# Reordering the loads and turns of the first two batches in an attention-and-MLP kernel

## The chip, the cores and the metric

The kernel runs on one core of a Trainium2 chip. The metric is device time in microseconds (us), the median of several executions. The profile's span, from the first to the last instruction, is about 1.7 us shorter than the time of its execution (303.1 and 301.4 for the kernel before).

Engines: PE is TensorE, DVE VectorE, ACT ScalarE, POOL GpSimd, SP SyncE, which here only issues transfers. PEld is PE's loading of weights. In a line of a profile, `L216` is a line of the kernel, `SPq` or `ACTq` an issue of a transfer by that engine, and the bracket says how long the engine was idle before and what ended that.

## The reference

```python
k_p = k.reshape(B, H, Sp, 8, D).mean(axis=3)      # keys pooled by 8; B=8, H=8, S=576, D=64
v_p = v.reshape(B, H, Sp, 8, D).mean(axis=3)
attn = softmax(q @ k_p.T / sqrt(D))               # 576 queries x 72 pooled keys a head
x = (attn @ v_p) reshaped to (4608, 512)
h = x @ w_in                                      # 512 x 2048
out = (h - tanh(h)) @ w_out                       # 2048 x 512
```

## The kernel before

The kernel works through eight batches. Attention of batch b+1 is slipped between the MLP matmuls of token group b. Only the start differs: batch 0's attention (the preamble) has no MLP to hide behind, and batch 1's attention, hidden behind the output matmuls of group 0, needs its data while all the weights are still loading.

k and v of a batch are 144 rows by 4 head pairs. 128 rows are loaded in one piece, and the 16 rows per pair left over (the "leftovers") separately. q is loaded as 4 x 128 rows, and its last 64 rows (the "small pieces", 512 runs of 256 B) separately. "Turning" is a transpose on PE by a matmul with the identity. `warm_pe` issues matmuls of zeros that only keep PE busy. The MLP's weights w_in and w_out (w1 and w2 in the code) are loaded in four pieces each. `KB` holds the turned keys, `VB` the pooled and masked values. AV is the product of the exponentials E with VB.

The preamble and the issue order of loads (cut):

```python
    load_main(k_pairs, k_raw[0], 0, 2, 4)      # SP queue
    load_q0(4, 8)                              # ACT queue
    load_dense(k_pairs, k_raw[0], 0)           # SP queue: leftovers
    load_dense(v_pairs, v_raw[1], 0)
    # ...
    for c in range(4):
        load_w1(c)                             # POOL queue, cast to bf16
    load_w2(0)
    nc.gpsimd.tensor_copy(out=v_bf[:, NM, :], in_=v_raw[1][:, NM, :])
    for c in range(1, 4):
        load_w2(c)
    # ...
    after(load_k(1), w1_dmas[1])               # k of batch 1 waits for the second w1 load
    load_q(1)                                  # main part and small pieces, SP queue
    load_main(v_pairs, v_raw[1], 1, 0, NM)
    # ...
    q_turn(nc.scalar.copy, 4, 6); q_turn(nc.scalar.copy, 6, 8)
    pool_k(0, nc.vector, 2, 4); pool_k(0, nc.vector, NM, NT)
    warm_pe(6)
    q_pe_transpose(0, (2, 3), "act")
    warm_pe(4)
    k_turn(2, 4)
    warm_pe(3)
    k_turn_left()
    v_left(...); vs = v_pe_pool(0, NM, ident); v_main(...)
    scores_wide(0, (NM, 2, 3))
```

Batch 1 behind the output matmuls of group 0 (cut):

```python
    pool_k(1, nc.gpsimd)
    q_cast(1)                                  # POOL
    after(load_k(2), w2_dmas[2])
    for u in range(16):
        qd, tb = u // 4, u % 4
        mlp_o(0, tb, qd * 4, qd * 4 + 4, gts, o_pools[tb])      # output block u
        if u == 0: k_transpose(1, ps_any)
        if u == 3: q_pe_transpose(1, (0, 1))
        # ... q turns at 4, 5; scores at 4 to 8
        if u == 7: pool_v(1, nc.vector)
        # u >= 9: AV of batch 1
```

The softmax here doesn't subtract the row's maximum and nothing guards it: scores larger than these inputs give would overflow.

## Time and profile before

| | |
|---|---|
| time | 303.22 us median (302.86 to 303.46, 4 runs) |
| span | 301.4 us |
| PE busy | 291.6 us, 97% |
| first output block of group 0 | 36.15 us |
| first AV of batch 1 | 49.01 us |
| first hidden block of group 1 | 57.31 us |

These three events cut the kernel into four stretches. The table of busy time has, for each stretch, its length, then busy time and instruction count of PE, PEld, DVE, ACT and POOL, and at the end the granted clock, the DMA share and GB/s. The second and third stretch before:

```profile
36.15:49.01 12.86, 11.75 (x83) 5.80 (x81) 6.88 (x11) 5.59 (x11) 2.49 (x2) 1.00 1.12 314
49.01:57.31 8.30, 8.26 (x74) 5.20 (x75) 6.41 (x23) 3.32 (x6) 7.07 (x4) 1.00 0.87 245
```

### The profile page before, as it was taken

To read this page: it belongs to the slowest core of one execution; us is meant where nothing else is said; L and a number is where in the kernel's file an instruction comes from. 1 tells how busy PE (TensorE), PEld (TensorE's weight loads), DVE (VectorE), ACT (ScalarE), POOL (GpSimd) and SP (SyncE) were. 2 spreads that over 40 slices of the span, in tenths; PEclk is the share of its full clock that TensorE was granted. 3 is DMA by queue.
4 is the path that set the end of the run, shared out by engine and by line. 5 is a ranking of instruction groups with operands and counts; after the bars stand their busy time and mean duration, and the time that the engine had idled before them with its cause. 6 is when DMAs were issued, how large, how long until landed. Compare 5 with 4: busy or idle time off the path is not lost.

```text
span 301.4 us, 4695 instructions
## 1 busy us (share of the span) xinstructions
PE 291.6 (97%) x1672; PEld 142.7 (47%) x1672; DVE 160.1 (53%) x344; ACT 146.4 (49%) x279; POOL 117.9 (39%) x112
## 2 busy tenths in 40 slices
PE   8789998999999999999999999999999999999994
PEld 3354454544554455445544554445444544444443
DVE  5567728685347524862577166807570757107600
ACT  5458642565426642665175506660675156226511
POOL 8701634871297109921991079408930000000000
PEclk9999999999999999999999999999999999999998
DMA  7999999649854896789657975795531430111032
GB/s 260 213 221 276 239 314 324 214 88 327 212 114 88 261 319 130 112 275 251 107 110 206 312 165 114 242 311 128 100 73 35 88 97 0 37 70 35 3 70 70
DMA packets 66183, 49.79 MB, mean 165 GB/s; under 512 B 39920, under 2 KB 52976, under 8 KB 66160
## 3 DMA queue, kind: packets, MB, share of 16 engines
q1 hardware_dynamic: 59520, 43.34, 54.5%
q0 software_dynamic: 4752, 4.72, 9.3%
q10 hardware_dynamic: 1888, 1.44, 1.8%
q8 instruction: 13, 0.21, 0.3%
q14 instruction: 10, 0.08, 0.1%
HBM read 36.70 MB, written 9.44 MB: 153 GB/s over the span
## 4 chain that ended last, share of the span: by engine, by line
PE 81%; DMA 14%; POOL 1%; DVE 1%; issue 0%; ACT 0%; SPq 0%; POOLq 0%
PE o_ps L449 37%; PE hT_ps L421 37%; DMA v_raw<-in_v_dram 6%; PE x_ps L339 4%; DMA w1b<-in_moe_w_in_dram 4%; DMA k_raw<-in_k_dram 3%; PE s_ps L291 3%; DMA out_dram<-o_sb 1%; DVE v_raw L209 0%; PE xT_ps L383 0%; POOL v_raw L569 0%; DVE v_raw L212 0%; DVE VB L223 0%; POOL w1b L496 0%; POOL mask L558 0%
## 5 line engine op out<-in xcount | busy, mean ns | idle before, releaser
L449 PE MATMUL o_ps<-w2b,gT 128*128 128x512 bf16 x560 | 134.4, 380 | 0.0
L434 DVE TENSOR_TENSOR gT<-hT_ps,t_sb 128x512 bf16<-128x512 f32 x144 | 98.9, 691 | 58.9 <-ACT t_sb L432 58.7
L421 PE MATMUL hT_ps<-xT,w1b 128*128 128x512 bf16 x576 | 127.0, 379 | 0.7 <-ACT xT L390 0.7
L432 ACT ACTIVATE t_sb<-hT_ps 128x512 f32<-128x512 f32 x144 | 85.6, 597 | 38.2 <-PE hT_ps L421 37.4
L421 PEld LDWEIGHTS <-w1b 128*128 128x128 bf16 x576 | 55.9, 98 | 66.9 <-issue 1.0
L449 PEld LDWEIGHTS <-gT 128*128 128x128 bf16 x560 | 52.5, 98 | 52.0 <-issue 1.4
L458 ACT COPY o_sb<-o_ps 128x512 f32<-128x512 f32 x33 | 19.3, 585 | 75.2 <-PE o_ps L449 75.2
L352 DVE RECIPROCAL rden<-x_ps 128x4 f32<-128x4 f32 x80 | 14.1, 177 | 50.5 <-PE x_ps L339 50.1
L144 POOL CAST q_bf<-q_raw 128x2048 bf16<-128x2048 f32 x7 | 13.2, 1888 | 62.7 <-DMA out_dram<-o_sb 23.6
L353 DVE TENSOR_TENSOR x_sb<-x_ps,rden 128x256 bf16<-128x256 f32 x80 | 34.0, 424 | 2.8
L193 POOL TENSOR_TENSOR k_raw<-k_raw 128x1280 f32<-128x1280 f32 x7 | 20.2, 2892 | 21.0 <-DMA k_raw<-in_k_dram 21.0
L310 ACT ACTIVATE E<-s_ps 128x288 bf16<-128x288 f32 x60 | 21.4, 410 | 13.2 <-PE s_ps L291 13.0
L339 PE MATMUL x_ps<-VB,E 128*128 128x130 bf16 x240 | 21.0, 221 | 1.1 <-DVE VB L223 1.1
L339 PEld LDWEIGHTS <-E 128*128 128x128 bf16 x240 | 16.9, 98 | 9.6 <-DVE VB L223 1.6
L209 POOL TENSOR_TENSOR v_raw<-v_raw 128x1280 f32<-128x1280 f32 x6 | 17.4, 2902 | 0.0
L291 PE MATMUL s_ps<-qT,KB 128*128 128x288 bf16 (+5 forms) x128 | 16.8, 290 | 0.0
L291 PEld LDWEIGHTS <-KB 128*128 128x128 bf16 (+1 forms) x128 | 7.0, 96 | 10.1 <-issue 3.4
L520 PE MATMUL warm_ps<-xT 128*128 128x512 bf16 x30 | 10.2, 463 | 1.3 <-DVE xT L532 1.3
L199 POOL TENSOR_TENSOR kd<-k_raw 128x640 bf16<-128x640 f32 x7 | 10.8, 1539 | 0.6
L196 POOL TENSOR_TENSOR k_raw<-k_raw 128x640 f32<-128x640 f32 x7 | 10.8, 1537 | 0.5
L390 ACT CAST xT<-xT_ps 128x256 bf16<-128x256 f32 (+1 forms) x14 | 6.0, 434 | 8.4 <-PE xT_ps L383 7.4
L212 POOL TENSOR_TENSOR v_raw<-v_raw 128x640 f32<-128x640 f32 x6 | 9.2, 1540 | 0.5
(73 smaller groups left out, 99.3 us busy)
## 6 DMA issues: line engine op xcount, KB each, us to landing
k_raw<-in_k_dram SPq DMA_DIRECT2D x7, 1024.0 KB, 5.8
q_raw<-in_q_dram SPq DMA_DIRECT2D x7, 1024.0 KB, 10.2
v_raw<-in_v_dram SPq DMA_DIRECT2D x7, 1024.0 KB, 8.9
out_dram<-o_sb SPq DMA_DIRECT2D x38, 128.0 KB, 2.5
out_dram<-o_sb SPq DMA_DIRECT2D x16, 256.0 KB, 2.6
w1b<-in_moe_w_in_dram POOLq DMA_DIRECT2D x4, 512.0 KB, 13.6
w2b<-in_moe_w_out_dram POOLq DMA_DIRECT2D x4, 512.0 KB, 26.8
k_raw<-in_k_dram SPq DMA_DIRECT2D x8, 128.0 KB, 6.0
```

What stands on the lines that cost most here:

```text
L193: first = eng.tensor_tensor(out=r[:, :, 0:4, :], in0=r[:, :, 0:4, :], in1=r[:, :, 4:8, :], op=ALU.add)
L209: eng.tensor_tensor(out=r[:, :, 0:4, :], in0=r[:, :, 0:4, :], in1=r[:, :, 4:8, :], op=ALU.add)
L291: nc.tensor.matmul(dst[p : p + w], lhsT=KB[b % 2][:, o : o + w], rhs=qTs[b][:, m, c0:c1], start=True, stop=True,)
L310: nc.scalar.activation(out=E[:, t, half * hs : (half + 1) * hs], in_=ps[:, :], func=ACT.Exp, scale=SCALE)
L339: nc.tensor.matmul(ps[:, 2 * n : 2 * n + 2, :].rearrange("p h d -> p (h d)") if n < 2 else ps.rearrange("p (a s) d -> p a s d", s=2)[:, :, ...
L352: nc.vector.reciprocal(out=rden[:, :, :], in_=ps[:, :, D:D1])
L353: nc.vector.tensor_tensor(out=x_sb[:, half, :, :], in0=ps[:, :, 0:D], in1=rden[:, :, :].to_broadcast([128, 4, D]), op=ALU.mult,)
L421: nc.tensor.matmul(h_tiles[i][:, :], lhsT=w1b[:, fb, i * 128 : (i + 1) * 128], rhs=xT[:, fb, tok0 : tok0 + TG], start=(fb == 0), stop=(fb ...
L432: nc.scalar.activation(out=t_sb[:, :], in_=h_ps[:, :], func=ACT.Tanh)
L434: nc.vector.tensor_sub(out=gT[:, :], in0=h_ps[:, :], in1=t_sb[:, :])
L449: nc.tensor.matmul(o_ps[:, :], lhsT=gts[i][:, tb * 128 : (tb + 1) * 128], rhs=w2b[:, i, :], start=(i == 0), stop=(i == NHID - 1),)
L458: (nc.vector.tensor_copy if g == 0 and tb % 2 else nc.scalar.copy)(out=o_sb[:, :], in_=o_ps[:, :])
```

## The change

It has two halves. In the preamble, the leftovers of batch 0 are to load behind q, so that q comes sooner, and the second half of k is turned ahead of q. For batch 1, q's small pieces go to the ACT queue, two weight loads are deferred into the pooling of k, q is cast on ScalarE, and the order of the turns follows. Cut to its core:

```diff
-    load_dense(k_pairs, k_raw[0], 0)
-    load_dense(v_pairs, v_raw[1], 0)
+    load_dense(k_pairs, k_raw[0], 0, nc.scalar)
+    load_dense(v_pairs, v_raw[1], 0, nc.scalar)
-    for c in range(1, 4):
-        load_w2(c)
+    load_w2(1)
-    load_q(1)
+    load_q(1, False)                     # without the small pieces
     pool_k(0, nc.vector, 2, 4)
+    warm_pe(6)
+    k_turn(2, 4)
     pool_k(0, nc.vector, NM, NT)
-    warm_pe(6)
+    warm_pe(2)
     q_pe_transpose(0, (2, 3), "act")
-    warm_pe(4)
-    k_turn(2, 4)
-    warm_pe(3)
+    warm_pe(2)
+    scores_wide(0, (2, 3))
     k_turn_left()
     # leftover scores now ahead of v's pooling; two warm_pe(2) more
     load_left(v_pairs, v_raw[1], 1, nc.scalar)
+    load_q_tail(1, q_raws[1], nc.scalar)
+    x_pe_transpose(0, 2, xs[2], (2, 4))
+    x_pe_transpose(0, 3, xs[3], (2, 4))
     mlp_h_mms(0, 3, 0, 2, (ps_o, "o_ps"))
-    x_pe_transpose(0, 2, xs[2], (2, 4))
     mlp_h_mms(0, 4, 0, 2, (ps_o, "o_ps"))
-    x_pe_transpose(0, 3, xs[3], (2, 4))
-    pool_k(1, nc.gpsimd)
-    q_cast(1)
+    pool_k(1, nc.gpsimd, mid=(2, 3))     # w2 loads 2 and 3 issued behind its first add
         if u == 0:
-            k_transpose(1, ps_any)
+            q_cast(1, nc.scalar.copy, 2)
+        if u == 2:
+            k_transpose(1, ps_any, (nc.vector.tensor_copy, nc.vector.tensor_copy))
         # q turns evicted by ACT alone; pool_v(1) at u == 4 instead of 7
```

More of the change, by code (lines that the diff above doesn't have):

```diff
@@ L108, in load_left, with load_dense @@
         ]
-    def load_dense(src, dst, b):
-        return nc.sync.dma_start(
+    def load_dense(src, dst, b, eng=nc.sync):
+        return eng.dma_start(
             out=dst[0 : NM * LO, NM, :], in_=src[b, 128:PR, :, :]
@@ L124, in load_v, with load_q_tail, load_q, q_cast @@
         )
-    def load_q(b, nh=1):
-        t = raw.tile([128, H, R + 1, D], FP32, name="q_raw", tag="q_raw")
-        n = H // nh
-        for i in range(nh):
-            nc.sync.dma_start(
-                out=t[:, i * n : (i + 1) * n, 0:R, :],
-                in_=q[b, i * n : (i + 1) * n, 0:QA, :].rearrange("h (p j) d -> p h j d", j=R),
-            )
-        nc.sync.dma_start(
+    def load_q_tail(b, t, eng):
+        eng.dma_start(
             out=t[:QT, :, R, :], in_=q[b, :, QA:S, :].rearrange("h p d -> p h d")
         )
-        q_raws[b] = t
+    def load_q(b, tail=True):
+        if b not in q_raws:
+            q_raws[b] = raw.tile([128, H, R + 1, D], FP32, name="q_raw", tag="q_raw")
+        t = q_raws[b]
+        nc.sync.dma_start(
+            out=t[:, :, 0:R, :], in_=q[b, :, 0:QA, :].rearrange("h (p j) d -> p h j d", j=R)
+        )
+        if tail:
+            load_q_tail(b, t, nc.sync)
     qTs = {}
     kdups = {}
-    def q_cast(b):
+    def q_cast(b, eng=nc.gpsimd.tensor_copy, parts=1):
         t = q_raws.pop(b)
-        nc.gpsimd.tensor_copy(
-            out=q_bf[:, 0:R, :, :].rearrange("p j h d -> p h j d"), in_=t[:, :, 0:R, :]
-        )
-        nc.gpsimd.tensor_copy(out=q_bf[:QT, R, :, :], in_=t[:QT, :, R, :])
+        n = H // parts
+        for h in range(0, H, n):
+            eng(
+                out=q_bf[:, 0:R, h : h + n, :].rearrange("p j h d -> p h j d"),
+                in_=t[:, h : h + n, 0:R, :],
+            )
+        eng(out=q_bf[:QT, R, :, :], in_=t[:QT, :, R, :])
     def q_dma_transpose(b):
@@ L185, in q_pe_tail, with pool_k @@
         evac(qTs[b][:, :, QA:S], ps[:, :, :])
-    def pool_k(b, eng, t0=0, t1=NT):
+    def pool_k(b, eng, t0=0, t1=NT, mid=()):
         r = k_raw[b % 2].rearrange("p t (j d) -> p t j d", d=D)[:, t0:t1, :, :]
@@ L195, in pool_k @@
         )
+        for c in mid:
+            load_w2(c)
         eng.tensor_tensor(
@@ L258, in turn_tile, with k_transpose @@
         )
-    def k_transpose(b, alloc):
+    def k_transpose(b, alloc, engs=(nc.vector.tensor_copy, nc.scalar.copy)):
         kd = kdups.pop(b)
@@ L264, in k_transpose @@
             turn_tile(ps[:, t, :], kd, t)
-        kb_main(KB[b % 2], ps, 0, NM, (nc.vector.tensor_copy, nc.scalar.copy))
+        kb_main(KB[b % 2], ps, 0, NM, engs)
         ps = alloc([128, 128], FP32, "kT_ps")
@@ L583 @@
     nc.gpsimd.memset(KB[1][:, :], 0.0)
+    q_raws[1] = raw.tile([128, H, R + 1, D], FP32, name="q_raw", tag="q_raw")
     after(load_k(1), w1_dmas[1])
-    load_q(1)
+    load_q(1, False)
     load_main(v_pairs, v_raw[1], 1, 0, NM)
@@ L636 @@
     pool_k(0, nc.vector, 2, 4)
+    warm_pe(6)
+    k_turn(2, 4)
     pool_k(0, nc.vector, NM, NT)
-    warm_pe(6)
+    warm_pe(2)
     q_pe_transpose(0, (2, 3), "act")
-    warm_pe(4)
-    k_turn(2, 4)
-    warm_pe(3)
+    warm_pe(2)
+    scores_wide(0, (2, 3))
     k_turn_left()
-    v_left(VB[0], v_pe_pool(NM, NT, spread)[:, 0, :, :], nc.vector)
+    warm_pe(2)
+    v_ps = v_pe_pool(NM, NT, spread)
+    scores_wide(0, (NM,))
+    v_left(VB[0], v_ps[:, 0, :, :], nc.vector)
     vs = v_pe_pool(0, NM, ident)
@@ L647 @@
     v_main(VB[0], vs, nc.vector, 2, 4)
-    scores_wide(0, (NM, 2, 3))
     load_left(v_pairs, v_raw[1], 1, nc.scalar)
+    load_q_tail(1, q_raws[1], nc.scalar)
     xs = [new_x() for _ in range(4)]
@@ L706 @@
         if u == 0:
-            k_transpose(1, ps_any)
+            q_cast(1, nc.scalar.copy, 2)
+        if u == 2:
+            k_transpose(1, ps_any, (nc.vector.tensor_copy, nc.vector.tensor_copy))
         if u == 3:
-            q_pe_transpose(1, (0, 1))
+            q_pe_transpose(1, (0, 1), "act")
         if u == 4:
-            q_pe_transpose(1, (2,))
+            q_pe_transpose(1, (2,), "act")
+            pool_v(1, nc.vector)
         if u == 5:
-            q_pe_transpose(1, (3,))
+            q_pe_transpose(1, (3,), "act")
         if 4 <= u <= 8:
             scores_wide(1, (u - 4,))
-        if u == 7:
-            pool_v(1, nc.vector)
         if u == 6:
```

## The prediction

> **What bounds the kernel now.** I read the shares by engine first, then the busy time by stretch, then the chain that ended last, then the DMA queues in windows along that chain.
>
> The table of busy time in four stretches (start, length, then PE, PEld, DVE, ACT, POOL busy, clock, DMA share, GB/s):
>
> ```profile
> 0.00:22.87 22.87, 18.32 (x125) 9.32 (x126) 13.42 (x43) 11.61 (x24) 12.03 (x29) 1.00 1.06 232
> 22.87:49.01 26.14, 24.71 (x158) 11.95 (x157) 17.20 (x30) 15.33 (x29) 8.48 (x5) 1.00 1.13 288
> 49.01:57.31 8.30, 8.26 (x74) 5.20 (x75) 6.41 (x23) 3.32 (x6) 7.07 (x4) 1.00 0.87 245
> 57.31:301.40 244.09, 240.30 (x1318) 116.23 (x1315) 123.08 (x250) 116.18 (x221) 90.34 (x75) 1.00 0.56 143
> ```
>
> From 57.31 us (token group 1) PE is solid, and no edited line lies there. The diff can only move the start of that stretch. Before it, PE's 18.32 us up to 22.87 contain 10.2 us of warm-up matmuls (30 of them, group list). So batch 0's preamble holds useful time to win, and the middle has 1.43 us without matmuls (26.14 - 24.71).
>
> The chain that ended last says what sets 49.01 (start, length, what):
>
> ```profile
> 5.85 12.31 DMA w1b<-in_moe_w_in_dram
> 18.18 10.21 DMA k_raw<-in_k_dram
> 28.41 16.92 DMA v_raw<-in_v_dram
> 45.34 1.50 DVE v_raw L209
> 48.26 0.70 DVE VB L223
> 49.01 0.29 PE x_ps L339 x2
> ```
>
> A shorter preamble alone therefore gains almost nothing: attention of batch 1 waits at 49.01 for VB, made 3.67 us after v of batch 1 lands (45.32). PE would arrive early and wait. The question is whether v, and what precedes it, arrives earlier too.
>
> The queues in windows 22:28, 28:36, 36:40, 42:44 (packets, MB, share of 16 engines; q0 is POOL's, q1 SP's):
>
> ```profile
> q0 software_dynamic: 581, 0.58, 56.7%
> q1 hardware_dynamic: 577, 1.14, 56.2%
> ...
> q0 software_dynamic: 979, 0.97, 71.4%
> q1 hardware_dynamic: 982, 1.00, 45.0%
> ...
> q0 software_dynamic: 601, 0.60, 88.0%
> q1 hardware_dynamic: 603, 0.22, 32.5%
> ...
> q1 hardware_dynamic: 395, 0.78, 101.1%
> ```
>
> SP carries k, then q, then q's small pieces (512 packets of 256 B), then v; POOL carries weights until 42. With both queues full they move equal numbers of packets, so 256 B packets hold a whole turn. From 36 to 40 SP moves only 0.22 MB; then v gets through at 0.39 MB/us because the weights have ended.
>
> **What the Trainium skill says.** (1) "DMA: Bandwidth & Descriptors", Queues, rings and completion order: each DMA engine round-robins between queue rows packet by packet. The trace agrees: 577 against 581, 982 against 979, 603 against 601. (2) Same page, Issuing engines are not separate DMA queues: another issuing engine saves only issue time. So moving a load to ACT removes no bytes, it changes whose turn they take. The windows agree: the sum stays near all engines' full share. (3) "ScalarE: Activation LUTs", What ACT_TABLE_LOAD costs: an ACTIVATE with immediates takes 186 ns + 0.833 ns per element. For 512 elements that is 0.61 us; the casts of q here take 0.57 to 0.62. Estimate for 1024 elements: 1.04 us alone, about 1.0 in a row. (4) "GPSIMD Engine Reference", Engine selection: one-input work is roughly line-rate there. It agrees: POOL's cast of 2048 elements takes 1.89 us. ACT's two halves take about the same; only the first half is ready sooner.
>
> **Part 1, dense leftovers of k and v behind q (ACT queue).** 2 x 128 KB = 128 packets of 2 KB leave SP's queue. In 6:8 SP moved 248 packets and ACT 240, and 33 of SP's came after 8. q's last half (512 KB) landed at about 10.4. Without about 95 of these before 8 and 33 after, estimate 0.5 + 0.2 us of engine time and a half instead of a third share for q: it lands at about 9.3, gain 1.1. Two issues on ACT (about 0.6 each, as on SP) push the table load and the first cast of q from 4.36 to about 5.1. Harmless: ACT reaches its first qT eviction at 6.31 anyway, after the second cast, which waits for its load until 5.78. The leftovers land at about 10.1 and 10.8 instead of 8.5 and 9.3.
>
> **Part 2, second k half turned ahead of q.** Its pooled keys are ready at 9.31, its turn waits behind q until 12.79. It goes to about 9.35, DVE evicts to 10.3. Then two casts of q 9.35 to 10.5, qT evictions to 11.6, scores 2 and 3 at 11.1 and 11.6 with their Exp to 12.7; pooled leftover keys at 11.5, their turn at 11.9; leftover scores at 12.6 (now 14.81). Of the 15 warm matmuls between the first two scores and AV, 14 remain (0.22 us each), mostly in waits; their number decides little. Pooling of v on PE then ends at about 13.9 and VB's first part is ready at about 14.4, against AV at 16.01: gain 1.6. v's cast load, landing near 12.4, just doesn't bind.
>
> **Part 3, x turns 2 and 3 ahead of hidden blocks 3 and 4.** It hides the turns' eviction behind eight matmuls: the 0.46 us gap at 22.87 goes, estimate 0.5. ACT's extra issue (0.71, from the like load of batch 0) ends before the first x eviction. So the MLP of group 0 starts about 2.1 us earlier, and PE alone would be at AV of batch 1 at 47.73 - 2.1 = 45.6, gain at most 3.4.
>
> **Part 4, q's small pieces on ACT, two w2 loads later.** The pieces now share turns from about 18 to 22 and slow POOL's weights and perhaps k's gate (w1's second load, 18.18) by up to 0.5. k lands at about 28.9 (28.4), q at about 37.9 (37.5), v behind it without the 4 us of small packets: 512 packets at 95 per us, the rate of 22:28, takes 5.4 us, 36.9 to 42.3. v lands near 42.7 instead of 45.3, partly because 2 us worth of w2 falls behind it. Both late w2 loads are issued near 33, before POOL's queue runs dry (35.4, w2's second), so they land near 41 and 44.5, needed at about 43 and 48. VB is ready at 42.7 + 3.7 = 46.4.
>
> POOL loses q's cast but pays 1.5 us of issues inside the pooling of k: keys ready at 37 or so (35.34). PE reaches the key turn after block 2 at 36.6, so it waits half a microsecond there.
>
> **Part 5, q's cast on ACT.** q lands at 37.9; cast halves 1.04 + 1.0, small pieces 0.55, eviction of the first qT 0.58, all in order on ACT: the first scores of batch 1 start at 37.9 + 3.3 = 41.2. They start at 41.41 now. From there PE was solid to 47.7, 6.3 us: AV at 47.5. This is later than VB (46.4) and than PE alone (45.6), so it binds. Gain 49.01 - 47.5 = 1.5; with q landing half a microsecond earlier, 2.0. Sum for the whole kernel, since the rest moves along rigidly: 1.7, that is 303.06 - 1.7 = 301.4.
>
> **Rivals.**
> A. PE-bound: q and v come early enough, the preamble gain shows in full. For it: the DMA share before 20 us could fall with the leftovers reordered. Against: k is still gated on w1's second load, and q still queues behind k. Time: 303.1 - 3.4 = 299.7.
> B. The small pieces in ACT's queue delay k and q by over a microsecond, and ACT's serial casts hold up the scores. For it: those packets hold whole turns (603 against 601). Against: they run mostly before k starts. Time: 302.5 to 303.5.
> C. The later w2 loads arrive too late for blocks 8 to 12, or delay k of batch 2, which waits for one of them (39.19 now). Block 8 is at 45.2 now. For it: they now share turns with v. Against: about 2 us of slack by Part 4, and scores of batch 2 come only at 73. Time: about 302.5.
> D. The expected case: q's landing and ACT's casts take over from v, 301 to 302.
>
> **Range and chances.** D gets most, A and B the tails: 300.1 to 302.7. Two per cent is 6.1 us, beyond the 3.4 us at most on offer; slower by that much would need a broken steady stretch.
>
> **What would show it.** Right: last half of q cast near 9.3; key turn near 9.4; leftover scores near 12.6; AV of batch 0 near 14.4; no gap before the second halves of the hidden blocks (near 20.8); v landing near 42.7; an ACT-bound gap before the first scores of batch 1 near 41.2; group 1 starting near 55.6 (57.31); and then the same 244.1 us. Wrong, if the first half of the preamble does not move (then PE order, not q, was the wait), if q of batch 1 lands before 37 or after 38.5, if PE waits for w2, or if the last stretch changes length by over 0.5 us.

## More of the kernel before

In the second stretch PE is busy 11.75 of 12.86 us. The missing 1.11 us is one wait, at its end, for VB:

```profile
49.01 0.72 PE L339 MATMUL x_ps<-VB,E 128*128 128x130 bf16 x6 [1.11 <-DVE VB L223]
```

On two of the chips used here the executions of one kernel scattered by 1 to 5 us, mostly upwards, which limits what small differences can say. That is noted where it matters.

## The result, and the profile after

The changed kernel takes 300.86 us (300.74 to 301.06, 4 runs), the kernel before 303.22 on the same occasion. The ratio is 0.9924, 95% interval 0.9907 to 0.9941: 2.4 us less, within 2%. Ratios compare fast runs of both kernels made together, so they are not quite the ratio of the quoted medians. A repeat on another chip gave 300.88 us and 0.9925.

The four stretches of the changed kernel, cut at the same events:

```profile
0.00:34.55 34.55, 31.25 (x200) 15.29 (x201) 23.84 (x63) 21.11 (x41) 15.01 (x30) 1.00 1.10 244
34.55:46.88 12.33, 11.81 (x82) 5.81 (x81) 6.17 (x10) 8.74 (x15) 3.13 (x3) 1.00 1.09 287
46.88:54.98 8.10, 8.10 (x75) 5.15 (x74) 6.15 (x22) 3.32 (x6) 5.97 (x3) 1.00 1.06 295
54.98:299.10 244.12, 240.29 (x1318) 116.25 (x1315) 122.96 (x250) 116.19 (x221) 91.34 (x75) 1.00 0.59 145
```

The saving adds up exactly: 36.15 - 34.55 = 1.60 us in the first stretch, 12.86 - 12.33 = 0.53 in the second, 8.30 - 8.10 = 0.20 in the third, and 244.09 to 244.12 in the last: 2.3 of the 301.4 us. The second stretch still has 0.52 us without matmuls (12.33 - 11.81). The old wait of 1.11 is gone and a new one of 0.52 has come.

What that new wait is, the chain that ended last tells (start, length, what):

```profile
5.86 12.86 DMA w1b<-in_moe_w_in_dram
...
19.21 10.84 DMA k_raw<-in_k_dram
...
30.21 2.90 POOL k_raw L198
33.11 1.47 POOL w2b L510 x2
34.58 1.58 POOL k_raw L203
36.23 1.55 POOL kd L206
37.82 0.45 PE kT_ps L259 x5
```

The wait itself, and DVE's start on v, in the timelines:

```profile
37.82 0.45 PE L259 MATMUL kT_ps<-ident,kd 128*128 128x128 bf16 x5 [0.52 <-POOL kd L206]
40.79 1.49 DVE L216 TENSOR_TENSOR v_raw<-v_raw 128x1280 f32<-128x1280 f32 x1 [1.47 <-DMA v_raw<-in_v_dram]
```

v has left the chain. Now k of batch 1 arrives at 30.05, POOL pools it in three adds, and in the middle sit the two w2 issues that the change put there. PE turns the keys at 37.82, as soon as they are ready. The issues are not all of it: POOL started on k at 29.21 before and at 30.21 now. From 35.34, when the keys were ready before, 1.0 us of later k and 1.4 of issues lead to 37.77.

The queues in windows 34:36, 36:38 and 38:40 show why v has left (packets, MB, share):

```profile
q1 hardware_dynamic: 576, 0.74, 101.7%
q0 software_dynamic: 27, 0.02, 5.9%
q1 hardware_dynamic: 314, 0.63, 85.1%
q0 software_dynamic: 75, 0.08, 22.5%
q0 software_dynamic: 360, 0.37, 109.8%
q1 hardware_dynamic: 55, 0.09, 13.5%
```

From 34 to 38 POOL's queue (q0) is nearly empty: w2's second load landed at 35.7, and the late ones, issued from 33.1 on, move nearly nothing before 37. SP's queue has the engines to itself and moves 1.37 MB in these 4 us. In the same four windows of time before (34 to 38), q0 kept moving 0.12 to 0.16 MB in every microsecond. DVE can start on v at 40.79 instead of 45.34.

And in the preamble, ACT's timeline around the first x evictions (start, length, what, idle before):

```profile
13.23 1.76 ACTq L106 DMA_DIRECT2D v_raw<-in_v_dram  x4
16.28 0.62 ACTq L127 DMA_DIRECT2D q_raw<-in_q_dram  x1
16.95 0.92 ACT L397 CAST xT<-xT_ps 128x256 bf16<-128x256 f32 x3 [3.19 <-PE x_ps L346]
```

The issue of the small pieces (L127) does not follow the four loads of v at 15.0 but waits until 16.28, and the first x eviction stands behind it in ACT's order. Batch 0's own small pieces landed at 16.2 (issued at 8.12, 8.1 to landing). The trace shows the times; the reason is read in the built program, where this issue waits for the completion counter (DMAHW0) which those pieces raise. The build gives such transfers one of eight counters, and makes a transfer wait for the earlier one that has the same.

### The profile page after: what moved, and what is told of

Its sections match the earlier page's. It is cut to its first block, busy times and chain, and to the rows that moved or that the text cites. A ratio compares the mean times of both kernels' runs of the same rounds, so it can differ in the third digit from the quotient of the medians.

```text
span 299.1 us, 4694 instructions
## 1 busy us (share of the span) xinstructions
PE 291.5 (97%) x1671; PEld 142.5 (48%) x1671; DVE 159.1 (53%) x343; ACT 149.4 (50%) x283; POOL 115.5 (39%) x110
## 4 chain that ended last, share of the span: by engine, by line
PE 85%; DMA 9%; POOL 4%; issue 0%; SPq 0%; ACT 0%; DVE 0%; POOLq 0%
PE o_ps L456 40%; PE hT_ps L428 37%; DMA w1b<-in_moe_w_in_dram 4%; PE x_ps L346 4%; DMA k_raw<-in_k_dram 4%; PE s_ps L298 3%; POOL k_raw L198 1%; DMA out_dram<-o_sb 1%; POOL k_raw L203 1%; POOL kd L206 1%; POOL w2b L510 0%; PE xT_ps L390 0%; POOL v_raw L576 0%; PE qT_ps L171 0%; POOL w1b L503 0%
## 5 line engine op out<-in xcount | busy, mean ns | idle before, releaser
L439 ACT ACTIVATE t_sb<-hT_ps 128x512 f32<-128x512 f32 x144 | 85.6, 597 | 38.3 <-PE hT_ps L428 37.5
L148 POOL CAST q_bf<-q_raw 128x2048 bf16<-128x2048 f32 x6 | 11.3, 1888 | 59.9 <-issue 34.8
```

What stands on the lines that cost most here:

```text
L439: nc.scalar.activation(out=t_sb[:, :], in_=h_ps[:, :], func=ACT.Tanh)
```

## The experiments

Theory after reading the two traces: the two halves of the change remove two waits in series, and neither pays in full without the other. A shorter preamble alone runs into v. An earlier v alone leaves PE late. With both, the pooling of k binds. The main rival is that each part has its own share and the shares add. A second rival says that the ACT queue, not the hole in the weights' queue, is what saves v. All twelve runs gave correct results. The medians of the kernel before were 303.47, 303.76 and 303.41.

**The preamble's edits alone.** Everything for batch 1 is as before:

```diff
-    load_w2(1)
+    for c in range(1, 4):
+        load_w2(c)
-    load_q(1, False)
+    load_q(1)
-    load_q_tail(1, q_raws[1], nc.scalar)
-    pool_k(1, nc.gpsimd, mid=(2, 3))
+    pool_k(1, nc.gpsimd)
+    q_cast(1)
     # and k_transpose, q turns, pool_v at their old places
```

> Only the preamble's edits (leftovers behind q, second k half ahead of q, the two x turns ahead); everything for batch 1 as before. My theory, two waits in series: group 0's output blocks start 1.6 us earlier or a little more (34.2 to 34.6 instead of 36.15), but v of batch 1 still lands at 45 to 45.5, so AV of batch 1 starts at 48.7 to 49.2 and the kernel gains 0 to 0.4 us (302.8 to 303.3). Rival, the gains add: the preamble's 1.6 us show in full, 301.6.

302.63 us, ratio 0.9962 (0.9922 to 1.0001), by the medians 0.84 less than before. The profile fell on one of the slower of its six executions (303.23). DVE's first add of v and PE's first AV of batch 1 there:

```profile
45.47 1.49 DVE L216 TENSOR_TENSOR v_raw<-v_raw 128x1280 f32<-128x1280 f32 x1 [0.76 <-DMA v_raw<-in_v_dram]
49.13 0.72 PE L346 MATMUL x_ps<-VB,E 128*128 128x130 bf16 x6 [0.34 <-DVE VB L230]
```

The output blocks start at 35.60, yet AV starts at 49.13, no sooner than before: v sets it. So the mechanism is as expected, with one wait more: PE also stood 1.07 us for q's cast on POOL before q's turns, and v cost it only the last 0.34. The sizes are not as expected: in this execution the second half of k came late (PE waited 1.73 us for its pooled keys), so the preamble gained only 0.55 us. The median gained more than the 0.4 at most that I had allowed. Why is open, as no faster execution was profiled. None of the six executions (lowest 302.4) reaches the 301.6 of adding gains, though the interval is too wide to exclude it.

**The edits for batch 1 alone.** The preamble is put back:

```diff
-    load_dense(k_pairs, k_raw[0], 0, nc.scalar)     # and v: back to SP
+    load_dense(k_pairs, k_raw[0], 0)
     # second half of k turned behind q, x turns behind blocks 3 and 4, as before
```

> Only the edits for batch 1 (small pieces of q on the ACT queue, two w2 loads inside the pooling of k, q cast on ScalarE, its order); the preamble as before. My theory: output blocks start at 36.1, pooled keys are ready at about 37.8 and PE reaches the key turn at 38.7, so it does not wait; v lands near 41, the wait of 1.1 us and the 0.2 us behind it go: gain 1.2 to 1.5 (301.7 to 302.0). Rival, adding gains: 0.7 us, as the whole change gives 2.4 and the preamble 1.6.

320.61 us (317.41 to 322.3), 17 us slower: both theories failed. The profiled execution counts as slow (322.3, clock 0.968), but the fast ones are 13.9 us or more above the kernel before as well. ACT's timeline:

```profile
29.53 0.62 ACTq L127 DMA_DIRECT2D q_raw<-in_q_dram  x1
30.19 0.92 ACT L397 CAST xT<-xT_ps 128x256 bf16<-128x256 f32 x3 [11.10 <-DMA k_raw<-in_k_dram]
```

The issue of the small pieces now waits from 19.85, when the loads of v ahead of it are issued, until 29.53, right after k of batch 1 lands (18.41 + 11.09 = 29.50), and ACT, PE and DVE wait behind it. In this build the issue waits for counter DMAHW1, which POOL's first add of k waits for too: the small pieces share a counter with k of batch 1, where in the changed kernel they share it with batch 0's small pieces. No line of the load itself differs. The hole is about 10 us. A part of the rest comes later: DVE's first multiplication for VB takes 3.83 us beside POOL's adds, against 0.69 in the kernel before. The granted clock is lower too: 0.73 from 16 to 31 us and 0.68 from 64.29 to 75, where two of the output blocks take 1.71 us each instead of 0.86; all six executions have a mean clock of 0.968 to 0.973. How the remaining microseconds divide I did not pursue.

**The same, mended.** The small pieces stay on SP, so nothing on ACT can wait for k:

```diff
-    load_q(1, False)
+    load_q(1)
-    load_q_tail(1, q_raws[1], nc.scalar)
```

> The run with batch 1's edits alone, mended: there the issue of q's small pieces on ACT waited from 19.9 to 29.5 us on the counter that k of batch 1 shares with it, and held ACT; here the small pieces stay on SP's queue, all else as in that run (late w2 loads, q cast on ScalarE, its order; preamble as before). My theory: output blocks start at 36.1 again, no 10 us hole, PE reaches the key turn at 38.7 after the keys are pooled, v lands at 41.5 to 43.5, AV of batch 1 at 47.5 to 48: gain 1.1 to 1.5 us against the kernel before. Rival, that something else in the late loads or the casts cost the 18 us: still far slower than before. Second rival, adding gains: 0.7 us.

303.46 us (302.14 to 304.25), ratio 0.9977 (0.9925 to 1.003): the 17 us were the wait for the shared counter and what followed from it. The profiled execution was the fastest, 302.14: output blocks at 36.58, DVE starts on v at 41.84, no wait at the key turn or before AV, which starts at 48.22, 0.8 us before 49.01, and group 1 at 56.31, 1.0 us before 57.31. So v's wait is gone as expected, and PE, coming late from its preamble, now sets the time. The size is not settled: the median gains 0.3, the profile 1.0, and this chip scattered by 2 us for this kernel. By medians, the halves alone give 0.84 and 0.30, together 2.36 to 2.53: they do not add, they need each other. By how much is open, as the intervals of both halves reach from no gain to over 2 us.

**The weights early again.** All of the change except the late w2 loads:

```diff
-    load_w2(1)
+    for c in range(1, 4):
+        load_w2(c)
-    pool_k(1, nc.gpsimd, mid=(2, 3))
+    pool_k(1, nc.gpsimd)
```

> The changed kernel with the two w2 loads issued in the preamble again, nothing else. My theory, that the hole of 34 to 37.5 us in the weights' queue is what lets q and v through: the hole is gone, q of batch 1 lands at 37.5 to 38 instead of 36.5, v at 42.5 to 44 instead of 40.8; keys are pooled 1.5 us sooner (36.3), but the first scores of batch 1 wait for q's casts until about 41: 0.3 to 0.8 us slower than the changed kernel (301.2 to 301.7). Rival, that moving the small pieces alone freed v and the late loads only hold up the pooling: 0.5 us faster (300.4).

302.61 us, against 300.86 and 300.88 for the changed kernel. It was run at another time. So about 1.7 us of the gain hang on the deferred loads by medians, and 1.2 by the profiled executions (spans of 300.3 and 299.1), in both cases more than I expected. The next run, with the late loads, has 300.74. DVE's first add of v and PE's first AV:

```profile
44.21 1.49 DVE L216 TENSOR_TENSOR v_raw<-v_raw 128x1280 f32<-128x1280 f32 x1 [6.00 <-DMA v_raw<-in_v_dram]
47.87 0.72 PE L346 MATMUL x_ps<-VB,E 128*128 128x130 bf16 x6 [0.48 <-DVE VB L230]
```

There is no hole: q0 moves 0.24 and 0.23 MB in 34:36 and 36:38. q lands so late that PE waits 1.15 us for ScalarE's cast before q's turns, and v again sets AV. The pooling of k was early enough not to matter. This is the wait which the prediction had put last, and it comes about just without the hole.

**The small pieces back on SP.** The changed kernel with

```diff
-    load_q(1, False)
+    load_q(1)
-    load_q_tail(1, q_raws[1], nc.scalar)
```

> The changed kernel with q's small pieces of batch 1 back in SP's queue behind q. My theory: they pass cheaply in the hole of the weights' queue, v lands 1 to 2 us later (42 to 43), still before it is needed (VB by 46.5, AV at 46.9); the first x eviction is no longer held by an issue on ACT, so the output blocks start 0.3 to 0.5 sooner; k lands earlier too, keys are pooled at 37.0 to 37.5: same to 0.6 us faster than the changed kernel (300.3 to 300.9). Rival, that the ACT queue is what saves v: v lands after 44, AV waits, 0.5 us or more slower (301.4 and up).

300.74 us, ratio 0.9912 (0.987 to 0.9955): as fast as the changed kernel. v is 1.1 us later (DVE starts at 41.89), which does not matter. The first x eviction comes at 15.80 instead of 16.95, the output blocks at 34.00 instead of 34.55, and PE's wait for the pooled keys grows from 0.52 to 0.78: about half of the 0.55 us gained is handed back there (group 1 starts at 54.69 instead of 54.98). So the move of the small pieces to the ACT queue, the edit with the clearest motive, is worth nothing here; in the profiles it costs 0.3 us. The rival that credits v to the ACT queue falls.

**q cast on POOL again.** The changed kernel with

```diff
     pool_k(1, nc.gpsimd, mid=(2, 3))
+    q_cast(1)
     # ...
-            q_cast(1, nc.scalar.copy, 2)
```

> The changed kernel with q of batch 1 cast on POOL behind the pooling of k. My theory: the cast starts at 37.8 when the pooling ends and gives q at 39.7, PE reaches q's turns at 39.0: it waits 0.7 us, so 0.6 to 0.8 us slower than the changed kernel (301.5). Rival, that v or the preamble binds and the cast has slack: the same time.

301.47 us (kernel before 303.76). PE waits twice:

```profile
37.89 0.45 PE L259 MATMUL kT_ps<-ident,kd 128*128 128x128 bf16 x5 [0.50 <-POOL kd L206]
39.73 0.62 PE L171 MATMUL qT_ps<-ident,q_bf 128*128 128x128 bf16 x8 [0.52 <-POOL q_bf L148]
```

Group 1 starts at 55.69 instead of 54.98: the cast on ScalarE is worth 0.7 us in the profiles and 0.6 by medians, as expected, because it takes the cast out of POOL's order behind the issues. The ratio, 0.9914 (0.987 to 0.9959), is too wide to tell it from the changed kernel's 0.9924.

**The late loads behind the pooling.** The changed kernel with

```diff
-    pool_k(1, nc.gpsimd, mid=(2, 3))
+    pool_k(1, nc.gpsimd)
+    for c in (2, 3):
+        load_w2(c)
```

> The changed kernel with the two late w2 loads issued behind the pooling of k instead of inside it. My theory, that PE's 0.52 us wait at the key turn is POOL's 1.5 us of issues: keys are pooled at about 36.3, the wait is gone, 0.4 to 0.6 us faster than the changed kernel (300.3), unless w2's third load now comes late for block 8 (reached at about 43.4; I expect it to land at 42.5 to 44), which would eat up to 0.5. Rival, that q's casts bind right behind: they end their first half at 37.6 and q's turns are reached at 38.4, so at most 0.2 gained.

300.92 us: not faster. But the wait at the key turn is gone, as expected, and group 1 starts at 54.45 instead of 54.98. The 0.53 us are given back in the stretch where nothing was edited:

```profile
85.83 13.97 PE L428 MATMUL hT_ps<-xT,w1b 128*128 128x512 bf16 x63 [0.41 <-DMA xT<-x_sb]
```

POOL starts pooling k of batch 2 only at 50.81 (48.56 in the changed kernel), and the whole chain of batch 2 slides with it (q cast at 57.38 instead of 55.96). That this delay is what holds the transposed x of group 2 is a reading of the order in SP's queue, not tested alone. It can't be the late cast by itself: with the small pieces on SP (two runs above) q is cast at 57.32, and the last stretch keeps its 244.0 us.

**Both at once.** Small pieces on SP, late loads behind the pooling (the last two diffs together).

> Both: w2 loads behind the pooling and small pieces on SP's queue. My theory: output blocks start at 34.0 as with the small pieces on SP alone, keys are pooled at about 36.0, before PE reaches them at 36.6: 0.7 to 0.9 us faster than the changed kernel (300.0), if w2's third load lands before PE reaches block 8 at about 43.2. Rival: it does not, PE waits there for 0.5 us or more, and the run equals the one with the small pieces on SP alone.

300.43 us (299.78 to 301.89), ratio 0.9886 (0.9838 to 0.9934). The output blocks start at 34.08, PE does not wait for the keys, group 1 starts at 54.12. The last stretch is 298.4 - 54.12 = 244.3 us, 0.2 longer than it should be. The median gain over the changed kernel is smaller than expected, on a scattering chip.

**Control.** The changed kernel again.

> The changed kernel unaltered, as the control of this call: 300.6 to 301.1.

300.88 us (300.58 to 301.4), as expected.

**A better split.** One late load inside the pooling, one behind it, small pieces on SP:

```diff
-    pool_k(1, nc.gpsimd, mid=(2, 3))
+    pool_k(1, nc.gpsimd, mid=(2,))
+    load_w2(3)
-    load_q(1, False)
+    load_q(1)
-    load_q_tail(1, q_raws[1], nc.scalar)
```

> Small pieces of q on SP's queue, one late w2 load inside the pooling of k, the other behind it. My theory: the keys are pooled 0.75 us sooner than with both inside, at about 36.8, when PE gets there; the first late load lands near 41, so k of batch 2 is not delayed as with both behind: group 1 starts at 53.9 to 54.2 and the last stretch keeps its 244.1 us: 0.6 to 0.9 us faster than the control. Rival, that q's landing and casts bind next: 0.3 us.

299.99 us (299.67 to 300.88), ratio 0.9897 (0.9882 to 0.9911), where the control has 0.9925 (0.9912 to 0.9938): 0.89 us faster than the changed kernel, 3.4 faster than before. This gain is that of the split and of the small pieces on SP together; the split was not run alone. POOL's timeline:

```profile
32.65 0.78 POOL L510 DMA_DIRECT2D w2b<-in_moe_w_out_dram  x1
33.45 1.56 POOL L203 TENSOR_TENSOR k_raw<-k_raw 128x640 f32<-128x640 f32 x1
35.08 1.54 POOL L206 TENSOR_TENSOR kd<-k_raw 128x640 bf16<-128x640 f32 x1
```

The keys are ready at 36.62 and PE turns them without a wait. Group 1 starts at 54.00, and the last stretch has its 298.1 - 54.00 = 244.1 us. Whether the split beats both loads behind the pooling is not shown: that run, also with the small pieces on SP, has a span of 298.4 against 298.1, and a ratio of 0.9886 against 0.9897. It was run at another time.

**The leftovers back on SP.** The changed kernel with both `load_dense` calls of batch 0 on SP's queue, nothing else.

> The changed kernel with the dense leftovers of batch 0 back on SP's queue. My theory: q's last half lands at 10.2 to 10.5 instead of 9.0, AV of batch 0 starts 0.6 to 1.0 later than 14.61; but ACT's issue of the small pieces still waits until about 16.2 and holds the first x eviction to about 16.9 anyway, and PE waits for the pooled keys: output blocks start 0 to 0.3 later, and the kernel is 0 to 0.2 us slower than the control. Rival, that each part's gain shows: 0.6 to 1.0 slower.

301.15 us, 0.27 more than the control. The casts of q's last half start at 10.92 instead of 9.00, AV of batch 0 at 16.11 instead of 14.49, the output blocks at 35.63 instead of 34.63. I expected those blocks only 0.3 us later at most; the preamble loses more. But PE then does not wait at the key turn, and only 0.46 of that 1.0 us reaches group 1 (55.37, control 54.91).

**The x turns back behind hidden blocks 3 and 4.**

```diff
-    x_pe_transpose(0, 2, xs[2], (2, 4))
-    x_pe_transpose(0, 3, xs[3], (2, 4))
     mlp_h_mms(0, 3, 0, 2, (ps_o, "o_ps"))
+    x_pe_transpose(0, 2, xs[2], (2, 4))
     mlp_h_mms(0, 4, 0, 2, (ps_o, "o_ps"))
+    x_pe_transpose(0, 3, xs[3], (2, 4))
```

> The changed kernel with the two x turns behind hidden blocks 3 and 4 again. My theory: the gap of 0.46 us before the second halves of the hidden blocks is back, output blocks start 0.5 to 0.6 later (35.1), PE's wait at the key turn (0.52) shrinks to 0 to 0.1: the kernel is 0 to 0.15 us slower than the control. Rival, that the reordering's gain shows: 0.5 slower.

301.03 us, 0.15 more than the control. The 0.46 us gap is back, output blocks start at 35.51 (34.63), later than the 0.6 us expected, and the wait at the key turn, 0.36 in the control, is gone. Here too much of the preamble's gain is swallowed by the pooling of k: group 1 starts at 55.24 (54.91).

The preamble's new order of turns and scores alone was not undone: put back with the small pieces on ACT it builds with the same counter as the run of 320 us.

## Why the prediction was right or wrong

The range held and the direction was clear of noise: 1.7 us forecast, 2.4 measured.

**Right.** That the preamble's gain would not pay unless v came earlier, that v would come earlier, and that everything from group 1 on would move rigidly: 244.09 and 244.12 us. The preamble's steps came as worked out: q's casts near 9.3 (8.98), the key turn near 9.4 (9.52), leftover scores near 12.6 (12.71), AV near 14.4 (14.61). The casts on ScalarE took the estimated two times about 1.0 (1.99 together). The half microsecond which PE would wait for the pooled keys is there, 0.52, but by luck: the keys were ready at 37.77 ("37 or so" thought) because k came 1.0 us later than before (0.5 thought), and PE, late from its preamble, got there at 37.3 (36.6 thought). Why k came later is open: POOL starts on it at 29.4 to 30.7 in all the runs, 29.21 before, and still at 29.91 with the small pieces on SP.

**Right in kind, wrong in weight: why v comes sooner.** Part 4 gave the removal of the small packets first and the weights falling behind v as a part. The runs turn this round: with the small pieces back on SP, DVE starts on v 1.1 us later (41.89), with the weights early 3.4 later (44.21).

**Wrong: "Both late w2 loads are issued near 33, before POOL's queue runs dry."** They were issued at 33.1 and 33.8, but nearly nothing of them moved until past 37, and the queue ran dry. I had taken the issue for the entry into the queue, though the trace of before already showed the first packets of POOL's queue only after 8, for an issue at 3.68. The delay is no constant: issued behind the pooling, at 35.97, the first packets came at 37.5. So q landed at 36.5, not 37.9, and v at 40.8, not 42.7. The run with early weights shows that the late loads, and with them this hole, carry 1.2 to 1.7 of the 2.4 us.

**Wrong in consequence: "This is later than VB (46.4) and than PE alone (45.6), so it binds"**, said of q's casts, and so the expected case D. By landing before 37, q gave one of the signs of being wrong that the prediction had named. With q 1.4 us earlier, the first scores of batch 1 started at 40.56, directly behind the matmuls before them. The pooling of k, which Part 4 had named and Part 5 covered up, was the wait that stayed. The runs with the loads behind it, or split around it, and the two that undid parts of the preamble all agree.

**Wrong: "ACT's extra issue (0.71, from the like load of batch 0) ends before the first x eviction."** It waited for a counter shared with batch 0's small pieces and held the eviction back from about 16.0 (0.32 after the turn at 15.70, as in the run without that issue) to 16.95. The output blocks started 1.60 us earlier, not 2.1. Of that miss 0.2 was AV of batch 0; with the issue off ACT the blocks started 2.15 earlier (34.00).

**The sum, term by term.** Preamble +1.60 (2.1 thought). Wait for VB +1.11 and the 0.20 behind it, both gone (thought gone too). Key turn -0.52 (thought covered by a larger wait). Wait for q's casts 0 (thought about 2). That makes 2.39; measured are 2.3 in the span.

**The rivals.** A, PE-bound, was nearly it: q and v did come early enough, and the best kernel here reaches 3.4 us, the most that it allowed. B had one part of it right: the small pieces did hold ACT, by a wait and not by their packets. C did not come in the changed kernel; its second half, a late k of batch 2, came when both w2 loads were pushed behind the pooling.

## What to carry to other kernels

When two waits lie in series, undo each part of a change alone before crediting it: here the halves alone gave 0.84 and 0.30 us of 2.4, and one edit with a good motive is worth nothing. Look for what an issue in an engine's program order makes wait, on both sides: two weight issues of 0.75 us each inside POOL's adds helped to make the new bound, and moving one of them behind the adds removed the wait without disturbing batch 2. A load put on a compute engine's queue can block that engine through a completion counter that the build shares with another load, so check in the built program which earlier transfer it waits for.

## What the Trainium skill lacked or had wrong

- "DMA: Bandwidth & Descriptors", Latency and other measured facts, gives about 1 us to the first byte of a load issued from GpSimd. Here the first packet came 4.1 us after the issue in the changed kernel (33.05 to 37.1), and 4.7 in the kernel before (3.68 to 8.4). Issued behind the pooling it took 1.5 (35.97 to 37.5), and 2.5 with the small pieces on SP (35.52 to 38.0). The long times belong to issues after which POOL had more work; that this is the cause was not tested. A prediction from the page's figure would be off by 3 us in the changed kernel.
- The same page, Why a DMA increments its semaphore by 16 and not by 1, advises one semaphore per transfer in flight. It lacks the price of sharing one where the build makes it safe by waiting: the issuing engine stood for 9.7 us (19.85 to 29.53) behind a transfer that had nothing to do with it, and the kernel lost 17 us.
